# Sparse attention with a SwiGLU FFN: scores of two heads in two row tiles, one-hot sums, a 0/1 mask multiplied by VectorE, and a written order of key-tile steps

## The chip, the cores and the metric

The kernel runs on one core of one Trainium2 chip. The metric is device time in microseconds (us) of that core. Engines are named as in the profile: PE is TensorE (PEld its weight loads), DVE is VectorE, ACT is ScalarE, POOL is GpSimd, SP is SyncE. Every time quoted for a kernel is the median of its runs; executions of one kernel mostly agree within half a per cent (those of e3, e6 and e14 below differ by 1.3 to 1.5).

## The reference

Four batches of block-sparse attention (8 heads, 768 tokens, head size 64), then one RMS norm and a SwiGLU FFN over the 3072 tokens. Blocks are of 32 tokens; a key block is visible if it is a neighbour, the first or last row or column, or one of three sampled blocks.

```
scores = q @ k.T / 8, masked to -1e9 where the block is not visible
attn   = softmax(scores) @ v                       # (4, 8, 768, 64)
x      = attn as (3072, 512)
xn     = x / sqrt(mean(x*x) + 1e-6) * rms_g
out    = (silu(xn @ w_gate) * (xn @ w_val)) @ w_out   # 512 -> 1536 -> 512
```

## The kernel before

The mask is part of the contraction of the scores: each head's K and Q have 24 more rows, an indicator of the key block and a row of 0 or -1000 for each query. Masked scores come out of one matmul of 88 rows, and the exponential makes them zero. V has a 65th column of ones, so the A·V matmul also gives the row sums.

```
def attn_head(b, h, stage, e):
    for jt in range(NC):                       # 6 key tiles
        for ic in range(2):                    # 2 halves of 384 queries
            stp = pst.tile([P, 384], FP32, tag="stp")
            nc.tensor.matmul(out=stp, lhsT=KTf[0:64 + NB, sl, jt*P:(jt+1)*P],
                             rhs=QTf[0:64 + NB, sl, ic*384:(ic+1)*384], ...)
            nc.scalar.activation(out=ExpS[:, sle, jt*2 + ic, :], in_=stp, func=AF.Exp, scale=SCALE)
    # ... 36 matmuls: ExpS as weights, V and its ones column (65) moving; then 1/Z, the scaling
    # and six sums of squares on VectorE

def ffn_gateval(pool, g, f):                   # gate and value of one 128-wide FFN tile
    gp = pool.tile([P, TG], FP32, tag="gp");  vp = pool.tile([P, TG], FP32, tag="vp")
    # ... 4 matmuls into gp, 4 into vp ...
    nc.scalar.activation(out=th, in_=gp, func=AF.Tanh, scale=0.5)
    nc.vector.scalar_tensor_tensor(out=u, in0=th, scalar=1.0, in1=gp, op0=ALU.add, op1=ALU.mult)
    nc.vector.tensor_tensor(out=hp, in0=u, in1=vp, op=ALU.mult)
# ... the FFN of batch b-1 is written between the heads of batch b; the last batch's FFN stands
# alone, with gp and vp in pools of two buffers each
```

The program's text gives only a rough order. The framework's scheduler decides in which order each engine gets its instructions.

The softmax here doesn't subtract the row's maximum and nothing guards it: scores larger than these inputs give would overflow.

Of the kernel before, what the change touches and what calls it, by code (L numbers as in the profile page):

```python
# [8 lines left out]

FP32 = mybir.dt.float32
BF16 = mybir.dt.bfloat16
# [6 lines left out]
def kernel(  # L19
# [13 lines left out]
    P = 128  # L33
# [5 lines left out]
    NT = B * S  # L39
    MASKV = -1000.0  # L40
    SCALE = 1.0 / (D ** 0.5)
    NRND = sampled_blocks.shape[1]
    NF = DFF // P
    TG = 384
    NTT = TG // P

    const = ctx.enter_context(tc.tile_pool(name="const", bufs=1))
    persist = ctx.enter_context(tc.tile_pool(name="persist", bufs=1))
    raw = ctx.enter_context(tc.tile_pool(name="raw", bufs=4))
    work = ctx.enter_context(tc.tile_pool(name="work", bufs=3))  # L50
    stg = ctx.enter_context(tc.tile_pool(name="stg", bufs=10))
    ffw = ctx.enter_context(tc.tile_pool(name="ffw", bufs=3))
    attn_psum_stack = ExitStack()
    pst = attn_psum_stack.enter_context(tc.tile_pool(name="pst", bufs=2, space=bass.MemoryType.PSUM))
    pt = attn_psum_stack.enter_context(tc.tile_pool(name="pt", bufs=1, space=bass.MemoryType.PSUM))
    po = attn_psum_stack.enter_context(tc.tile_pool(name="po", bufs=1, space=bass.MemoryType.PSUM))
    pff = attn_psum_stack.enter_context(tc.tile_pool(name="pff", bufs=1, space=bass.MemoryType.PSUM))
# [4 lines left out]
    epsb = const.tile([P, 1], FP32, name="epsb")  # L62
    nc.vector.memset(epsb, 1e-6)
# [5 lines left out]
        base=1, pattern=[[-1, 32]], channel_multiplier=1,  # L69
    )  # L70
    nc.gpsimd.affine_select(
        out=Bm, in_=Bm, compare_op=ALU.is_ge, fill=0.0,
        base=1, pattern=[[1, 32]], channel_multiplier=-1,
    )
    for cm, base in ((1, 0), (1, -(NB - 1)), (0, 0), (0, -(NB - 1))):
        pat = [[1, 32]] if cm == 0 else [[0, 32]]
        nc.gpsimd.affine_select(
            out=Bm, in_=Bm, compare_op=ALU.not_equal, fill=1.0,
            base=base, pattern=pat, channel_multiplier=cm,
        )  # L80
    samp_i = const.tile([32, NRND], I32, name="samp_i")
    _sbt = sampled_blocks.tensor
    _sbt32 = _dc.replace(_sbt, dtype=I32, shape=tuple(_sbt.shape[:-1]) + (_sbt.shape[-1] * 2,))
    s64 = _sbt32.ap()
    nc.sync.dma_start(out=samp_i[0:NB, :], in_=s64[:, 0:2 * NRND:2])
    samp_f = const.tile([32, NRND], FP32, name="samp_f")
    nc.vector.tensor_copy(out=samp_f[0:NB, :], in_=samp_i[0:NB, :])
    jb_iota = const.tile([32, 32], I32, name="jb_iota")
    nc.gpsimd.iota(jb_iota, pattern=[[1, 32]], base=0, channel_multiplier=0)
    jb_iotaf = const.tile([32, 32], FP32, name="jb_iotaf")  # L90
    nc.vector.tensor_copy(out=jb_iotaf, in_=jb_iota)
    onehot = const.tile([32, 32], BF16, name="onehot")
    for r in range(NRND):
        nc.vector.tensor_tensor(
            out=onehot[0:NB, 0:NB],
            in0=samp_f[0:NB, r:r + 1].to_broadcast([NB, NB]),
            in1=jb_iotaf[0:NB, 0:NB], op=ALU.is_equal,
        )
        nc.vector.tensor_tensor(
            out=Bm[0:NB, 0:NB], in0=Bm[0:NB, 0:NB], in1=onehot[0:NB, 0:NB],  # L100
            op=ALU.max,
        )
    BmT = const.tile([32, 32], BF16, name="BmT")
    nc.vector.transpose(out=BmT, in_=Bm)

    Kind = const.tile([32, S], BF16, name="Kind")
    nc.gpsimd.memset(Kind, 1.0)
    nc.gpsimd.affine_select(
        out=Kind[0:NB, :], in_=Kind[0:NB, :], compare_op=ALU.is_equal, fill=0.0,
        base=0, pattern=[[1, NB], [0, 32]], channel_multiplier=-1,  # L110
    )
    Qmask = const.tile([32, S], BF16, name="Qmask")
    bmt_exp = BmT[0:NB, 0:NB].to_broadcast([NB, NB, 32])
    nc.vector.tensor_scalar(
        out=Qmask[0:NB, :], in0=bmt_exp,
        scalar1=-MASKV, scalar2=MASKV, op0=ALU.mult, op1=ALU.add,
    )

    NSLOT = 6
    NSLOTE = 2  # L120
    KTf = persist.tile([P, NSLOT, S], BF16, name="KTf")
    QTf = persist.tile([P, NSLOT, S], BF16, name="QTf")
    Vp = persist.tile([P, NSLOT, NC, 65], BF16, name="Vp")
    ExpS = persist.tile([P, NSLOTE, 12, 384], BF16, name="ExpS")
    for sl in range(NSLOT):
        nc.scalar.dma_start(out=KTf[64:64 + NB, sl, :], in_=Kind[0:NB, :])
        nc.scalar.dma_start(out=QTf[64:64 + NB, sl, :], in_=Qmask[0:NB, :])
        nc.vector.memset(Vp[:, sl, :, 64:65], 1.0)

    xbr = [persist.tile([P, NT], BF16, name=f"xbr{i}") for i in range(DM // P)]  # L130
    ssq = persist.tile([P, 2, NC], FP32, name="ssq")
    rstd = persist.tile([P, 2, NC], FP32, name="rstd")

    rmsg = const.tile([P, H // 2], FP32, name="rmsg")
    nc.sync.dma_start(out=rmsg, in_=moe_rms_g.rearrange("(h p) -> p h", p=P))

    wg = persist.tile([P, DM // P, DFF], BF16, name="wg")
    wv = persist.tile([P, DM // P, DFF], BF16, name="wv")
    wo = persist.tile([P, NF, DM], BF16, name="wo")
    nc.gpsimd.dma_start(out=wg, in_=moe_w_gate.rearrange("(c p) f -> p c f", p=P))  # L140
    nc.gpsimd.dma_start(out=wv, in_=moe_w_val.rearrange("(c p) f -> p c f", p=P))
    nc.gpsimd.dma_start(out=wo, in_=moe_w_out.rearrange("(c p) f -> p c f", p=P))
    nc.scalar.mul(out=wo, in_=wo, mul=0.5)

    hprods = {}

    def ffn_gateval(pool, g, f):
        gp = pool.tile([P, TG], FP32, name="gp", tag="gp")
        vp = pool.tile([P, TG], FP32, name="vp", tag="vp")
        for c in range(DM // P):  # L150
            nc.tensor.matmul(  # L151
                out=gp, lhsT=wg[:, c, f * P:(f + 1) * P],
                rhs=xbr[c][:, g * TG:(g + 1) * TG],
                start=(c == 0), stop=(c == DM // P - 1),
            )
        for c in range(DM // P):
            nc.tensor.matmul(  # L157
                out=vp, lhsT=wv[:, c, f * P:(f + 1) * P],
                rhs=xbr[c][:, g * TG:(g + 1) * TG],
                start=(c == 0), stop=(c == DM // P - 1),  # L160
            )
        th = ffw.tile([P, TG], BF16, name="th", tag="th")
        nc.scalar.activation(out=th, in_=gp, func=AF.Tanh, scale=0.5)  # L163
        u = ffw.tile([P, TG], BF16, name="u", tag="u")
        nc.vector.scalar_tensor_tensor(  # L165
            out=u, in0=th, scalar=1.0, in1=gp, op0=ALU.add, op1=ALU.mult,
        )
        hp = ffw.tile([P, TG], BF16, name="hp", tag="hp", bufs=2 * NF + 2)
        nc.vector.tensor_tensor(out=hp, in0=u, in1=vp, op=ALU.mult)  # L169
        hprods[(g, f)] = hp  # L170

    def ffn_out(pool, g, tt):
        yp = pool.tile([P, DM], FP32, name="yp", tag="yp")
        for f in range(NF):
            nc.tensor.matmul(  # L175
                out=yp, lhsT=hprods[(g, f)][:, tt * P:(tt + 1) * P],
                rhs=wo[:, f, :],
                start=(f == 0), stop=(f == NF - 1),
            )
        yo = ffw.tile([P, DM], FP32, name="yo", tag="yo")  # L180
        nc.scalar.copy(out=yo, in_=yp)  # L181
        nc.sync.dma_start(out=out[g * TG + tt * P:g * TG + (tt + 1) * P, :], in_=yo)

    def make_ffn_units(b, pool):
        units = []
        for g in (2 * b, 2 * b + 1):
            for f in range(NF):
                units.append((ffn_gateval, pool, g, f))
            for tt in range(NTT):
                units.append((ffn_out, pool, g, tt))  # L190
        return units

    def attn_pair_load(b, hp):
        sl0 = (b * H + 2 * hp) % NSLOT
        sl1 = (b * H + 2 * hp + 1) % NSLOT
        qraw = raw.tile([P, NC, 2, D], FP32, name="qraw", tag="qraw")
        kraw = raw.tile([P, NC, 2, D], FP32, name="kraw", tag="kraw")
        for e in range(2):
            nc.sync.dma_start(  # L199
                out=qraw[:, :, e, :],  # L200
                in_=q[b, 2 * hp + e].rearrange("(c p) d -> p c d", p=P))
            nc.sync.dma_start(  # L202
                out=kraw[:, :, e, :],
                in_=k[b, 2 * hp + e].rearrange("(c p) d -> p c d", p=P))
        qbf = work.tile([P, NC, 2 * D], BF16, name="qbf", tag="qbf")
        kbf = work.tile([P, NC, 2 * D], BF16, name="kbf", tag="kbf")
        nc.vector.tensor_copy(out=qbf, in_=qraw)  # L207
        nc.vector.tensor_copy(out=kbf, in_=kraw)
        for e, (raw_, bf) in enumerate(((qraw, qbf), (kraw, kbf))):
            dst = QTf if e == 0 else KTf  # L210
# [125 lines left out]
```

## Time and profile before

| | before |
|---|---|
| time, median | 437.4 us (436.01 to 437.44), 436.78 with the run beside the changed kernel |
| TensorE, VectorE, ScalarE busy | 83%, 56%, 55% of the span |
| first exponential, first FFN matmul | 55.1 us, 131.3 us |
| from the end of the last exponential to the end | 64.8 us |

Part 1 of the profile's page: busy time of each engine, its share, and its instructions.

```profile
span 436.2 us, 7564 instructions
...
PE 360.2 (83%) x2854; PEld 209.8 (48%) x2880; DVE 246.4 (56%) x821; ACT 241.7 (55%) x518; POOL 6.2 (1%) x19
```

TensorE is the busiest. Its busy time by itself is no measure of work, since matmuls are pipelined (in the timeline below one is 0.33 us long, and the next starts after 0.163); what counts is how far apart they start. The table of windows divides the span by stage. Columns: the window and its length, busy us (and instructions) of PE, PEld, DVE, ACT and POOL, the granted TensorE clock, the DMA share, GB/s.

```profile
0.00:55.00 55.00, 6.44 (x44) 4.26 (x45) 14.69 (x43) 6.61 (x2) 6.17 (x19) 1.00 1.07 192
55.00:125.00 70.00, 60.30 (x444) 34.37 (x442) 32.22 (x149) 47.30 (x106) 0.00 (x0) 0.90 0.64 126
125.00:372.00 247.00, 237.46 (x2056) 140.91 (x2080) 164.82 (x559) 167.82 (x375) 0.00 (x0) 0.99 0.14 37
372.00:436.00 64.00, 56.02 (x317) 30.22 (x316) 34.71 (x71) 19.92 (x36) 0.00 (x0) 0.97 0.10 37
```

The clock's column has a gap: this profile's record of the clock starts only at 104.6 us, and earlier stretches are printed as 1.00. The chain of waits shows otherwise (start us, us, what):

```profile
60.91 1.89 PE opsum L246 x31
...
150.67 1.00 PE opsum L246 x31
```

The same 31 A·V matmuls start 0.055 us apart at 60.9 us and 0.032 at 150.7: the first batch's attention ran at a lower clock too, about half by this ratio.

Four stages: a start with little TensorE work, one batch of attention alone, a dense mixed stage (237.5 of 247 us busy), and a last stage of FFN alone.

The costliest groups, by form (columns: line, engine, operation, shapes, count; busy us and mean ns of one; idle us just before them, and whom they waited for):

```profile
L238 ACT ACTIVATE ExpS<-stp 128x384 bf16<-128x384 f32 x384 | 171.1, 491 | 48.4 <-PE stp L232 33.8 <-DMA QTf<-Qmask 8.3 <-PE opsum L246 2.7
L232 PE MATMUL stp<-QTf,KTf 88*128 88x384 bf16 x384 | 126.5, 365 | 15.4 <-ACT ExpS L238 9.4 <-DMA QTf<-Qmask 3.4 <-DVE KTf L214 0.6
...
L259 DVE CUSTOM_DVE_ANT_0 junk<-stage,ssq 128x64 bf16<-128x64 bf16 x168 | 36.6, 277 | 0.3
```

The last stage in the timeline (start us, us, engine, line, what):

```profile
396.03 0.33 PE L151 MATMUL gp<-xbr_152,wg 128*128 128x384 bf16 x1
396.11 0.56 DVE L165 SCALAR_TENSOR_TENSOR u<-th,gp 128x384 bf16<-128x384 bf16 x1
...
396.68 0.33 PE L157 MATMUL vp<-xbr_152,wv 128*128 128x384 bf16 x1
...
396.88 0.49 ACT L163 ACTIVATE th<-gp 128x384 bf16<-128x384 f32 x1 [0.81 <-PE gp L151]
...
397.33 0.33 PE L151 MATMUL gp<-xbr_152,wg 128*128 128x384 bf16 x1
```

One FFN tile takes 1.30 us there (gate matmuls start at 396.03 and again at 397.33), exactly eight matmuls of 0.163 us. The tanh and the multiply on VectorE run beside them, for another tile.

### The profile page before, as it was taken

To read this page: it belongs to the slowest core of one execution; us is meant where nothing else is said; L and a number is where in the kernel's file an instruction comes from. 1 tells how busy PE (TensorE), PEld (TensorE's weight loads), DVE (VectorE), ACT (ScalarE), POOL (GpSimd) and SP (SyncE) were. 2 spreads that over 40 slices of the span, in tenths; PEclk is the share of its full clock that TensorE was granted. 3 is DMA by queue.
4 is the path that set the end of the run, shared out by engine and by line. 5 is a ranking of instruction groups with operands and counts; after the bars stand their busy time and mean duration, and the time that the engine had idled before them with its cause. 6 is when DMAs were issued, how large, how long until landed. Compare 5 with 4: busy or idle time off the path is not lost.

```text
span 436.2 us, 7564 instructions
## 1 busy us (share of the span) xinstructions
PE 360.2 (83%) x2854; PEld 209.8 (48%) x2880; DVE 246.4 (56%) x821; ACT 241.7 (55%) x518; POOL 6.2 (1%) x19
## 2 busy tenths in 40 slices
PE   0002288898879999999999999989999999789996
PEld 0001134554555654655555555546555555345552
DVE  0016534363476862766887648578665566657380
ACT  0003266667676666676777476767773867333331
POOL 5000000000000000000000000000000000000000
PEclk9999999999659999999999999999999999989999
DMA  7999986557470202211310111010001000100101
GB/s 124 208 203 207 221 165 136 99 107 148 90 146 20 54 23 90 62 29 44 94 30 20 44 53 34 2 50 24 2 2 50 24 2 2 73 2 0 74 0 72
DMA packets 82407, 30.80 MB, mean 71 GB/s; under 512 B 76452, under 2 KB 78276, under 8 KB 82372
## 3 DMA queue, kind: packets, MB, share of 16 engines
q1 hardware_dynamic: 79332, 25.18, 26.1%
q0 software_dynamic: 2608, 4.72, 5.9%
q10 hardware_dynamic: 432, 0.44, 0.4%
q8 instruction: 22, 0.36, 0.4%
q14 instruction: 13, 0.11, 0.1%
HBM read 28.31 MB, written 6.29 MB: 79 GB/s over the span
## 4 chain that ended last, share of the span: by engine, by line
PE 71%; ACT 9%; SPq 8%; DVE 7%; DMA 3%; issue 2%; ACTq 0%; DVEq 0%
PE stp L232 17%; PE gp L151 14%; PE vp L157 13%; PE yp L175 13%; PE opsum L246 11%; ACT ExpS L238 7%; SPq L220 3%; SPq L202 3%; PE tqk L213 2%; PE to L280 2%; SPq L199 1%; DVE junk L259 1%; DMA vraw<-in_v_dram 1%; ACT yo L181 1%; DMA QTf<-Qmask 1%
## 5 line engine op out<-in xcount | busy, mean ns | idle before, releaser
L238 ACT ACTIVATE ExpS<-stp 128x384 bf16<-128x384 f32 x384 | 171.1, 491 | 48.4 <-PE stp L232 33.8
L232 PE MATMUL stp<-QTf,KTf 88*128 88x384 bf16 x384 | 126.5, 365 | 15.4 <-ACT ExpS L238 9.4
L165 DVE SCALAR_TENSOR_TENSOR u<-th,gp 128x384 bf16<-128x384 bf16 x96 | 53.0, 552 | 58.9 <-ACT th L163 56.5
L246 PE MATMUL opsum<-Vp,ExpS 128*128 128x65 bf16 x1152 | 76.8, 209 | 1.4 <-ACT ExpS L238 1.2
L246 PEld LDWEIGHTS <-ExpS 128*128 128x128 bf16 x1152 | 56.5, 107 | 44.3 <-issue 24.6
L163 ACT ACTIVATE th<-gp 128x384 bf16<-128x384 f32 x96 | 47.1, 490 | 54.2 <-PE gp L151 53.9
L175 PE MATMUL yp<-wo,hp 128*128 128x512 bf16 x262 | 65.6, 379 | 3.2 <-ACT yo L181 2.6
L169 DVE TENSOR_TENSOR hp<-u,vp 128x384 bf16<-128x384 bf16 x96 | 52.8, 551 | 19.3 <-PE vp L157 12.8
L232 PEld LDWEIGHTS <-KTf 88*128 88x128 bf16 x384 | 39.0, 107 | 30.5 <-issue 14.5
L151 PEld LDWEIGHTS <-wg 128*128 128x128 bf16 x384 | 35.8, 98 | 29.2 <-issue 7.9
L157 PEld LDWEIGHTS <-wv 128*128 128x128 bf16 x384 | 36.2, 98 | 25.2 <-issue 3.0
L213 PE MATMUL tqk<-ident,qbf 128*128 128x128 bf16 x96 | 13.0, 263 | 37.4 <-DVE qbf L207 37.3
L175 PEld LDWEIGHTS <-hp 128*128 128x128 bf16 x288 | 27.7, 97 | 32.2 <-issue 4.5
L181 ACT COPY yo<-yp 128x512 f32<-128x512 f32 x24 | 14.1, 586 | 42.7 <-PE yp L175 40.7
L259 DVE CUSTOM_DVE_ANT_0 junk<-stage,ssq 128x64 bf16<-128x64 bf16 x168 | 36.6, 277 | 0.3
L151 PE MATMUL gp<-xbr_152,wg 128*128 128x384 bf16 x96 | 31.6, 329 | 2.5 <-DVE u L165 1.7
L157 PE MATMUL vp<-xbr_152,wv 128*128 128x384 bf16 x96 | 31.6, 329 | 0.6 <-DVE hp L169 0.3
L151 PE MATMUL gp<-xbr_155,wg 128*128 128x384 bf16 x96 | 31.5, 329 | 0.1
L157 PE MATMUL vp<-xbr_153,wv 128*128 128x384 bf16 x96 | 31.6, 329 | 0.0
L151 PE MATMUL gp<-xbr_153,wg 128*128 128x384 bf16 x96 | 31.6, 329 | 0.0
L157 PE MATMUL vp<-xbr_154,wv 128*128 128x384 bf16 x96 | 31.4, 328 | 0.0
L157 PE MATMUL vp<-xbr_155,wv 128*128 128x384 bf16 x96 | 31.4, 328 | 0.0
(53 smaller groups left out, 235.0 us busy)
## 6 DMA issues: line engine op xcount, KB each, us to landing
qraw<-in_q_dram SPq DMA_DIRECT2D x32, 192.0 KB, 3.7
kraw<-in_k_dram SPq DMA_DIRECT2D x32, 192.0 KB, 4.0
vraw<-in_v_dram SPq DMA_DIRECT2D x32, 192.0 KB, 3.1
out_dram<-yo SPq DMA_DIRECT2D x24, 256.0 KB, 2.0
wg<-in_moe_w_gate_dram POOLq DMA_DIRECT2D x1, 1536.0 KB, 12.8
wv<-in_moe_w_val_dram POOLq DMA_DIRECT2D x1, 1536.0 KB, 18.8
wo<-in_moe_w_out_dram POOLq DMA_DIRECT2D x1, 1536.0 KB, 27.9
KTf<-Kind ACTq DMA_DIRECT2D x6, 36.0 KB
```

What stands on the lines that cost most here:

```text
L151: nc.tensor.matmul(out=gp, lhsT=wg[:, c, f * P:(f + 1) * P], rhs=xbr[c][:, g * TG:(g + 1) * TG], start=(c == 0), stop=(c == DM // P - 1),)
L157: nc.tensor.matmul(out=vp, lhsT=wv[:, c, f * P:(f + 1) * P], rhs=xbr[c][:, g * TG:(g + 1) * TG], start=(c == 0), stop=(c == DM // P - 1),)
L163: nc.scalar.activation(out=th, in_=gp, func=AF.Tanh, scale=0.5)
L165: nc.vector.scalar_tensor_tensor(out=u, in0=th, scalar=1.0, in1=gp, op0=ALU.add, op1=ALU.mult,)
L169: nc.vector.tensor_tensor(out=hp, in0=u, in1=vp, op=ALU.mult)
L175: nc.tensor.matmul(out=yp, lhsT=hprods[(g, f)][:, tt * P:(tt + 1) * P], rhs=wo[:, f, :], start=(f == 0), stop=(f == NF - 1),)
L181: nc.scalar.copy(out=yo, in_=yp)
L213: nc.tensor.transpose(out=t_[:, c, :], in_=bf[:, c, :], identity=ident)
L232: nc.tensor.matmul(out=stp, lhsT=KTf[0:64 + NB, sl, jt * P:(jt + 1) * P], rhs=QTf[0:64 + NB, sl, ic * 384:(ic + 1) * 384], start=True, sto ...
L238: nc.scalar.activation(out=ExpS[:, sle, jt * 2 + ic, :], in_=stp, func=AF.Exp, scale=SCALE,)
L246: nc.tensor.matmul(out=opsum[:, it, 0:65], lhsT=ExpS[:, sle, jt * 2 + it // 3, (it % 3) * P:(it % 3 + 1) * P], rhs=Vp[:, sl, jt, :], start ...
L259: nc.vector.tensor_tensor_reduce(out=junk, in0=stage[:, it, e, :], in1=stage[:, it, e, :], scale=1.0, scalar=(0.0 if h == 0 else ssq[:, b ...
```

## The change

The intent: half the exponential instructions (two heads, 768 wide), two heads' scores at the same time in two row tiles of TensorE, A·V in two column tiles, row sums as matmuls with one-hot weights, a shorter lag of the FFN behind the attention (units of 384 queries and not of 768), and an order written by hand, in which each of 192 steps takes one key tile of two heads and about 0.97 us of FFN work. (A row tile is half the rows of TensorE's array, enough for a contraction of 64; a column tile is half or a quarter of its columns.) The mask goes out of the contraction: a 0/1 tile is multiplied onto the exponentials by VectorE. The core of the diff (cuts marked):

```
+    ctx.enter_context(tc.manual_schedule())
...
+    def load_w_chunk(i):                        # norm weight folded into the gate and value weights
+        for w, src, mul in ((wg, wgv, 1.0), (wv, wvv, 0.5)):
+            st = wst.tile([P, DM // P, FCH], FP32, name="wstage", tag="wstage")    # 2 buffers
+            nc.sync.dma_start(out=st, in_=src[:, :, f0:f0 + FCH])
+            for c in range(DM // P):
+                nc.vector.tensor_scalar(out=w[:, c, f0:f0 + FCH], in0=st[:, c, :], ...)
...
+    def qk_exp(n, jt):
+        s_ = ps_s.tile([P, 2, 512], FP32, name="s_", tag="s")
+        for e in range(2):
+            nc.tensor.matmul(out=s_[:, e, 0:TG],
+                lhsT=KT[64 * e:64 * e + 64, jt * P:(jt + 1) * P],
+                rhs=QT[64 * e:64 * e + 64, ic * TG:(ic + 1) * TG], start=True, stop=True)
+        nc.scalar.activation(out=ptiles[n][:, jt, :, :], in_=s_[:, :, 0:TG], func=AF.Exp, scale=SCALE)
+        if jt % 2:
+            nc.vector.tensor_tensor(out=pv, in0=pv, in1=Mk[...].to_broadcast([P, 2, 2, TG]), op=ALU.mult)
...
+    # av: 12 matmuls in two column tiles; zsum: 12 in four column tiles of 32; wsum: sum of squares
+    # norm_a .. norm_d: 1/Z and 1/rms as matmuls, nine small VectorE operations, a GpSimd power
...
+    def ff_g(u, f):
+        if u == NU - 1:
+            gv = ps_s.tile([P, 2, 512], FP32, name="gv", tag="s")     # gate and value: two halves
+            gp = gv[:, 0, 0:TG]
+        else:
+            gp = ps_f.tile([P, TG], FP32, name="gp", tag="gp")        # one buffer
+        # 4 matmuls, tanh on ScalarE, uu on VectorE
+    def ff_v(u, f):
+        vp = ps_f.tile([P, TG], FP32, name="vp", tag="vp") if gv is None else gv[:, 1, 0:TG]
...
+        at(s1 + 4, norm_a, u); at(s1 + 5, norm_b, u); at(s1 + 6, norm_c, u)     # one step apart
+        at(s1 + 7, norm_d, u, 0); at(s1 + 7, norm_d, u, 1)
+    for i in range(DFF // FCH):
+        at(5 + 4 * i, load_w_chunk, i)
```

## The prediction

> **What bounds the kernel now.** TensorE. It is busy 83% of 436.2 us (page, part 1); the chain of waits is 71% TensorE. By stage (table of windows): to 55 us TensorE works 6 us (q arrives at 26.9 us; ScalarE's queue waits 40.1 us on the K-indicator copies); from 55 to about 125 us the first batch's attention runs without FFN; to 372 us it is mixed, TensorE 93-97% busy; from 372 us only the last batch's FFN is left, 64 us. In the timeline FFN matmuls start every 0.163 us (384 columns), the 512-column ones every 0.22, and 31 A·V matmuls take 1.0 us. Started work is thus: scores 384x0.163=63, A·V 38, FFN 125+63, transposes 192x0.1=19: 308 us. The mixed stage holds three batches of attention and FFN, some 228 us, in 247: already dense.
>
> **What changes (estimates from those durations).**
> TensorE: scores in row tiles 192x0.19=36, A·V in column tiles 192x0.18=35, new one-hot sums 18+5, 384 small transposes 20-25, norm matmuls 15, FFN the same 188: about 320 us. It does *not* shrink. The Trainium skill's "TensorEngine Tiling (Array Packing)", Key Properties, says that changing the tiling mode drains TensorE; each step now changes it at least twice. No line of this profile shows its cost; I allow 0.05-0.1 us each, 25-45 us in all, part of it hidden in other waits.
> ScalarE: 384 exponentials of 384 (0.45 apart) become 192 of 768 (0.45+384x0.83 ns=0.77): 171 to 148; but evictions of A·V and K add 29; Sqrt table loads and the 5.3 us scaling of wo go. In all about 240.
> VectorE: the squares (36.6+15.2), stage and casts go; mask multiplies come, 96x0.95=91 (1536 elements at two per cycle, as the 0.55 us casts show, plus 0.15), weight folding 11, norm 35. In all about 250, as before.
> Neither is the bound, but both stand in strict order in the FFN chain: gate matmuls, tanh 0.49, u 0.55, then the single gate bank is free. With exponentials and mask multiplies ahead in the queue that takes about 2 us, against 0.8-1.5 us of other TensorE work: waits of 3-6 us per unit. The norm chain (nine small VectorE ops and a GpSimd power) adds 2 us per unit.
>
> **Critical path.** Gain: scores start near 19 us instead of 50; FFN starts near 60 us instead of 125 (held there by VectorE waiting for four weight chunks, 6-8 us of DMA each); the tail has half a batch, about 37 us instead of 64. In between lie 160 steps at 1.68 us of TensorE work = 269 us; with drains and waits 1.8-2.05, 290-330 us.
> Sum: 60 + 290..330 + 37 = 387..427; the ideal is 366. I lean to the lower end since the order looks tuned.
>
> **Predicted: 388 us, 350 to 425. Faster by over 2%: 0.85; within 2%: 0.09; slower: 0.06.**
>
> **What would show it.** Exponentials of 128x768 near 0.8 us; mask multiplies near 0.95; paired score matmuls starting almost together; VectorE idle on weight DMAs between 25 and 55 us; gate matmuls waiting on u; step period 1.8-2.0 us; from the last exponential to the end 35-40 us.
>
> **What would make it wrong.** Tiles that don't run together (zsum, A·V: +80 us, slower than before); drains near zero and a well-hidden gate chain (350 or less); a slower start from software-queue DMAs; a mask multiply at one element per cycle (1.75 us, VectorE the bound).

## The result, and the profile after

Ratios here are the mean time of one kernel's fast runs over that of the other's of the same rounds, so they differ a little from the ratio of the medians quoted.

| | before | changed |
|---|---|---|
| time, median | 436.78 us (436.01 to 437.44) | 488.81 us (487.64 to 490.6) |
| ratio | 1 | 1.1201 (95%: 1.1172 to 1.1231) |
| first exponential, first FFN matmul | 55.1, 131.3 us | 18.0, 77.5 us |
| last exponential's end to the end | 64.8 us | 60.6 us |

The result is right; the kernel is 12% slower. The prediction, 388 us with a range of 350 to 425, was wrong.

Part 1 of the page, and the table of windows by the stages of the changed kernel (start, attention alone, mixed, FFN alone):

```profile
span 485.7 us, 6795 instructions
...
PE 378.1 (78%) x2742; PEld 172.0 (35%) x2742; DVE 253.1 (52%) x441; ACT 236.5 (49%) x369; POOL 74.1 (15%) x112
```

```profile
0.00:18.00 18.00, 7.28 (x40) 2.99 (x41) 9.82 (x16) 2.08 (x2) 15.72 (x40) 1.00 0.76 102
18.00:77.50 59.50, 35.12 (x274) 14.45 (x273) 32.91 (x65) 29.33 (x42) 12.33 (x18) 0.71 0.73 162
77.50:425.00 347.50, 296.44 (x2216) 135.37 (x2213) 190.06 (x321) 193.71 (x304) 44.33 (x54) 0.98 0.16 32
425.00:485.60 60.60, 39.29 (x219) 19.23 (x216) 20.33 (x40) 11.41 (x23) 1.67 (x2) 1.00 0.07 26
```

TensorE, the fullest engine, is busy for 85% of the mixed stage, where it was 96% before. The mixed stage takes 347.5 us for 160 steps, 2.17 us each (predicted 1.8 to 2.05); the two others, 77.5 and 60.6 us, were predicted at 60 and 37. In the second stage the recorded clock averages 0.71. The Trainium skill's "TensorE: Matmul & The Clock Gate", Part 1, says that TensorE runs at half clock until it has been busy for some 3.4 us and falls back after an idle window; the trace agrees as far as it goes: 34 of the 52.7 us that it records at half clock lie in this stage, where TensorE waits. The record starts at 29.0 us, so the 1.00 of the first stage is not a measurement, and the two kernels' totals can't be compared.

The groups that answer to those of before:

```profile
L249 DVE TENSOR_TENSOR pt<-pt,Mk 128x1536 bf16<-128x1536 bf16 x96 | 91.5, 957 | 99.8 <-ACT pt L245 95.9
...
L363 PE MATMUL gp<-xn,wg 128*128 128x384 bf16 x336 | 68.6, 326 | 21.2 <-DVE uu L369 19.9
...
L367 ACT ACTIVATE th<-gp 128x384 bf16<-128x384 f32 x84 | 41.3, 492 | 39.2 <-PE gp L363 38.8
```

The mask multiply took 957 ns, as estimated (0.95). The exponentials of 768 took 0.81 us each in the timeline and start 0.70 us apart when back to back. Single costs were right; the waits were not. The chain of waits in part 4, before and then changed, by engine:

```profile
PE 71%; ACT 9%; SPq 8%; DVE 7%; DMA 3%; issue 2%; ACTq 0%; DVEq 0%
```

```profile
PE 46%; DVE 20%; ACT 18%; issue 7%; DMA 4%; POOL 2%; POOLq 0%; DVEq 0%; ACTq 0%
```

Of the chain that ended last, TensorE was 71% and is 46%; VectorE and ScalarE went from 16 to 38%. The view of waits (who waited for whom: us in total, times, longest us):

```profile
DVE pt L249 <- ACT pt L245: 95.9, 53, 5.9
...
PE gp L363 <- DVE uu L369: 19.9, 31, 1.4
...
PE gv L377 <- DVE uu L369: 14.0, 12, 1.2
...
PE s__430 L241 <- ACT KT L229: 11.8, 1, 11.8
...
PE ft L330 <- DVE FHL_190 L323: 10.3, 4, 3.3
...
PE ft L330 <- DVE FHL_191 L323: 7.1, 4, 2.2
```

The lines from the second on are TensorE's: gate matmuls that wait for u (the only gate bank, the buffer that TensorE writes them to, is still read), value matmuls of the last unit that wait for u, one wait of 11.8 us at the start, and the norm's matmul. The first line says that VectorE stands at the head of its queue 96 us for exponentials.

**The norm chain.** Unit 5's, from VectorE's sums to TensorE's matmul:

```profile
282.55 0.87 POOL L317 TENSOR_TENSOR rs<-ms,nhalf 128x3 f32<-128x3 f32 x1 [8.44 <-DVE ms L314]
283.46 0.18 DVE L319 TENSOR_TENSOR fx<-rz,rs 128x24 f32<-128x24 f32 x1 [0.99 <-POOL rs L317]
...
283.89 0.18 DVE L323 TENSOR_TENSOR FHL_190<-fx,FHL_190 128x24 bf16<-128x24 f32 x1
...
284.13 0.34 PE L330 MATMUL ft<-ident,FHL_190 128*128 128x128 bf16 x3 [2.23 <-DVE FHL_190 L323]
```

TensorE stands 2.23 us before its three transposes: the written order left one step between the chain's start and its use.

**The tail.** The last stage of the changed kernel:

```profile
456.27 0.49 ACT L367 ACTIVATE th<-gv 128x384 bf16<-128x384 f32 x1 [2.14 <-PE gv L363]
456.79 0.56 DVE L369 SCALAR_TENSOR_TENSOR uu<-th,gv 128x384 bf16<-128x384 bf16 x1 [0.62 <-ACT th L367]
457.40 0.81 PE L377 MATMUL gv<-xn,wv 128*128 128x384 bf16 x4 [1.17 <-DVE uu L369]
...
458.05 0.81 PE L363 MATMUL gv<-xn,wg 128*128 128x384 bf16 x4
...
458.89 0.49 ACT L367 ACTIVATE th<-gv 128x384 bf16<-128x384 f32 x1 [2.14 <-PE gv L363]
459.42 0.55 DVE L369 SCALAR_TENSOR_TENSOR uu<-th,gv 128x384 bf16<-128x384 bf16 x1 [0.62 <-ACT th L367]
```

One FFN tile now takes 2.63 us (u starts at 456.79 and at 459.42), where the same eight matmuls took 1.30 before. The value matmuls start 0.05 us after u has ended (456.79 + 0.56), although they don't need u: they write the other half of the tile whose first half u reads. Twelve tiles at 1.33 us too much are 16 us.

**The start.** VectorE from 25 to 45 us:

```profile
31.93 1.41 DVE L210 TENSOR_SCALAR wg<-wstage,gcol 128x384 bf16<-128x384 f32 x4 [6.02 <-DMA wstage<-in_moe_w_gate_dram]
...
38.18 1.41 DVE L210 TENSOR_SCALAR wv<-wstage,gcol 128x384 bf16<-128x384 f32 x4 [4.85 <-DMA wstage<-in_moe_w_val_dram]
39.51 1.82 DVE L249 TENSOR_TENSOR pt<-pt,Mk 128x1536 bf16<-128x1536 bf16 x2
41.24 0.55 DVE L228 COPY QT<-tqk 128x768 bf16<-128x768 bf16 x1
```

It waits 6.0 and 4.9 us for weight chunks; a mask multiply and the eviction of Q (L228, which the copy of K on ScalarE follows) stand behind, and TensorE waits 11.8 us for that copy.

**Mode changes.** Full-array gate matmuls, the scores' row tiles, full-array value matmuls, with nothing to wait for:

```profile
255.89 0.33 PE L363 MATMUL gp<-xn,wg 128*128 128x384 bf16 x1
...
256.15 0.34 PE L241 MATMUL s__2645<-QT,KT 64*128 64x384 bf16 x2
...
256.42 0.82 PE L377 MATMUL vp<-xn,wv 128*128 128x384 bf16 x4
```

The two score matmuls (x2) run at once: a run of 0.34 us is the length of one. But from the last gate matmul to them it is 0.26 us, and from them to the value matmuls 0.27, where a full-array matmul of 384 columns takes 0.163. So each change of tile mode costs 0.10 us. The Trainium skill's "TensorEngine Tiling (Array Packing)", Key Properties, says that a change of mode drains TensorE and gives no time; the trace agrees that it costs TensorE time, and by kind of change the median of those without a wait is 0.095 to 0.107 us.

**TensorE's account.** I took the starts of successive matmuls, counted 0.163 us for 384 columns (0.216 for 512) once for tiles that start together, 0.10 for each change of mode, and the rest as waiting:

| stretch | streaming | mode changes | waiting |
|---|---|---|---|
| before, mixed stage, 125 to 372 us | 210 us (85%) | none seen | 36 us (15%) |
| changed, units 5 to 8, 215 to 424 us | 142 us (68%) | 24 us (11%), 239 changes | 43 us (21%) |

A quarter of the second stretch, about one unit of 24 steps, is 52.3 us: 35.5 of streaming, 6.0 of changes, 10.8 of waiting. Over the whole span the same count gives some 293 us of streaming and 112 of waiting before, and 289 of streaming, 43 of mode changes (443) and 140 of waiting in the changed kernel.

### The profile page after: what moved, and what is told of

Same layout as the page of the kernel before. It is cut to its first block, busy times and chain, and to the rows that moved or that the text cites. A ratio compares the mean times of both kernels' runs of the same rounds, so it can differ in the third digit from the quotient of the medians.

```text
span 485.7 us, 6795 instructions
## 1 busy us (share of the span) xinstructions
PE 378.1 (78%) x2742; PEld 172.0 (35%) x2742; DVE 253.1 (52%) x441; ACT 236.5 (49%) x369; POOL 74.1 (15%) x112
## 4 chain that ended last, share of the span: by engine, by line
PE 46%; DVE 20%; ACT 18%; issue 7%; DMA 4%; POOL 2%; POOLq 0%; DVEq 0%; ACTq 0%
ACT pt L245 11%; PE yp L391 11%; DVE pt L249 7%; PE gp L363 7%; PE vp L377 6%; DVE uu L369 4%; PE zw L282 3%; ACT th L367 3%; DMA wstage<-in_moe_w_val_dram 3%; PE gv L377 2%; DVE hp L380 2%; ACT yo L397 2%; PE gv L363 2%; PE fb L344 1%; DVE QT L228 1%
## 5 line engine op out<-in xcount | busy, mean ns | idle before, releaser
L249 DVE TENSOR_TENSOR pt<-pt,Mk 128x1536 bf16<-128x1536 bf16 x96 | 91.5, 957 | 99.8 <-ACT pt L245 95.9
L363 PE MATMUL gp<-xn,wg 128*128 128x384 bf16 x336 | 68.6, 326 | 21.2 <-DVE uu L369 19.9
L377 PE MATMUL vp<-xn,wv 128*128 128x384 bf16 x336 | 68.6, 327 | 5.4 <-DVE hp L380 5.4
L369 DVE SCALAR_TENSOR_TENSOR uu<-th,gp 128x384 bf16<-128x384 bf16 x84 | 46.4, 552 | 47.8 <-ACT th L367 47.5
L380 DVE TENSOR_TENSOR hp<-uu,vp 128x384 bf16<-128x384 bf16 x84 | 46.4, 553 | 13.8 <-PE vp L377 9.4
L241 PEld LDWEIGHTS <-KT 64*128 64x128 bf16 x384 | 19.5, 94 | 85.7 <-issue 84.7
L229 ACT COPY KT<-tqk 128x768 bf16<-128x768 bf16 x16 | 12.8, 798 | 44.0 <-DVE QT L228 44.0
L264 PEld LDWEIGHTS <-vb 128*64 128x64 bf16 x384 | 21.5, 119 | 20.2 <-issue 12.0
L282 PE MATMUL zw<-pt,Ez 128*32 128x384 bf16 x384 | 22.9, 347 | 0.0
L347 DVE TENSOR_TENSOR xn<-osb,fb 128x768 bf16<-128x768 f32 x16 | 14.5, 948 | 1.5 <-PE fb L344 1.5
L380 DVE TENSOR_TENSOR hp<-uu,gv 128x384 bf16<-128x384 bf16 x12 | 6.6, 554 | 10.8 <-PE gv L377 10.8
```

What stands on the lines that cost most here:

```text
L241: nc.tensor.matmul(out=s_[:, e, 0:TG], lhsT=KT[64 * e:64 * e + 64, jt * P:(jt + 1) * P], rhs=QT[64 * e:64 * e + 64, ic * TG:(ic + 1) * TG] ...
L249: nc.vector.tensor_tensor(out=pv, in0=pv, in1=Mk[:, jt - 1:jt + 1, ic * TG:(ic + 1) * TG].unsqueeze(2).to_broadcast([P, 2, 2, TG]), op=ALU ...
L264: nc.tensor.matmul(out=o_[64 * e:64 * e + 64, 0:TG], lhsT=vb[:, 2 * pr + e, jt * D:(jt + 1) * D], rhs=pt_[:, jt, e, :], start=(jt == 0), s ...
L282: nc.tensor.matmul(out=zwt[u][32 * c:32 * c + 32, :], lhsT=Ez[:, pr, :], rhs=pt_[:, 2 * j2 + par, e, :], start=(pr == 0 and j2 == 0), stop ...
L363: nc.tensor.matmul(out=gp, lhsT=wg[:, c, f * P:(f + 1) * P], rhs=xns[u][:, c, :], start=(c == 0), stop=(c == NP - 1))
L369: nc.vector.scalar_tensor_tensor(out=uu, in0=th, scalar=1.0, in1=gp, op0=ALU.add, op1=ALU.mult)
```

## The experiments

Sixteen runs, three rounds each (the last two five). Theory: the parts of the change cost what they were said to cost, and the loss lies in new waits, made by the written order and by shared buffers, and in mode changes. Rivals: VectorE's mask work itself; row tiles; the written order as such; waits that hide one another, so that mending them gives nothing. Ratios are to the kernel before; the changed kernel has 1.1201.

| run | median us | ratio (95%) |
|---|---|---|
| e1 tail tiles apart | 471.9 | 1.0827 (1.0801 to 1.0853) |
| e2 norm later | 467.29 | 1.0718 (1.0701 to 1.0735) |
| e3 mask multiply later | 471.05 | 1.0798 (1.0741 to 1.0855) |
| e4 the scheduler's order | 438.67 | 1.0077 (1.0038 to 1.0117) |
| e5 336 more mode changes | 513.15 | 1.176 (1.1731 to 1.1789) |
| e6 its control | 494.4 | 1.1334 (1.127 to 1.1397) |
| e7 full-array scores | 510.49 | 1.1729 (1.1668 to 1.1791) |
| e8 no mask multiply (wrong result) | 455.87 | 1.0449 (1.0428 to 1.047) |
| e9 control of e7 | 511.81 | 1.1731 (1.1667 to 1.1795) |
| e10 weights early | 480.12 | 1.102 (1.0969 to 1.1071) |
| e11 four mends, written order | 417.58 | 0.9589 (0.9547 to 0.9631) |
| e12 scheduler, mended | 430.5 | 0.989 (0.9853 to 0.9926) |
| e13 e11 with the additive mask | 417.85 | 0.959 (0.9557 to 0.9624) |
| e14 e11 without a mask (wrong result) | 407.51 | 0.9361 (0.9334 to 0.9388) |
| e15 the kernel of e9 again | 511.07 | 1.1718 (1.1688 to 1.1748) |
| e16 the kernel of e7 again, same chip | 511.7 | 1.1738 (1.1712 to 1.1765) |

All but e8 and e14 gave the right result. The medians of e8 and e9 include one slow run each (463.73 and 530.38 us; without them 455.31 and 511.59); the ratios use fast runs alone.

### e1: tail tiles apart

```
-        if u == NU - 1:
-            gv = ps_s.tile([P, 2, 512], FP32, name="gv", tag="s")
-            gp = gv[:, 0, 0:TG]
+        if u == NU - 1 and f % 2:
+            gp = ps_s.tile([P, 2, 512], FP32, name="g2", tag="s")[:, 0, 0:TG]
+            gv = ps_s.tile([P, 2, 512], FP32, name="v2", tag="s")[:, 0, 0:TG]
         else:
             gp = ps_f.tile([P, TG], FP32, name="gp", tag="gp")     # value: the bank of vp
```

Two FFN tiles may be under way at once, as in the changed kernel; only gate and value are no longer halves of one tile.

> Changed kernel, but in the last unit gate and value go to separate tiles, alternating between the two FFN banks and the two score tiles. Main theory (of the 100 us miss, the tail's share is a dependency of the value matmuls on u, because both halves of one tile count as one; the tail then runs 2.63 us per FFN tile where the kernel before ran 1.30): period near 1.30 us, last exponential to end 60.5 -> 45 us, total 489 -> 473 +-3. Rival (the tail is bound by TensorE or by the tanh/u latency itself, not by the shared tile): period stays above 2.2 us, total within 3 us of 489.

It took 471.9 us, 17 less. VectorE's u in its tail:

```profile
445.68 0.55 DVE L370 SCALAR_TENSOR_TENSOR uu<-th,g 128x384 bf16<-128x384 bf16 x1
...
446.98 0.55 DVE L370 SCALAR_TENSOR_TENSOR uu<-th,gp 128x384 bf16<-128x384 bf16 x1
```

u comes every 1.30 us (445.68, 446.98). The last exponential ends at 425.9 and the kernel at 470.5: 44.6 us and not 60.6. The shared tile cost 16 to 17 us.

### e2: norm later

```
-            at(s1 + 6, norm_c, u);  at(s1 + 7, norm_d, u, 0);  at(s1 + 7, norm_d, u, 1);   LAG = 8
+            at(s1 + 8, norm_c, u);  at(s1 + 9, norm_d, u, 0);  at(s1 + 9, norm_d, u, 1);   LAG = 10
```

> Changed kernel with the last two parts of the norm chain emitted two steps later (FFN lag 10 instead of 8 steps). Main theory (TensorE stands 2.2 us per unit at the transpose matmul of the norm, waiting for nine small VectorE operations and the GpSimd power): that wait falls below 0.3 us per unit in seven units, and the total falls by 8-14 us; the last unit has nothing to fill the gap with. Rival (the gap is only moved: TensorE would wait elsewhere, on exponentials or on u, anyway): total within 4 us of 489.

It took 467.29 us, 21.5 less and more than I had expected. The view of waits no longer lists the norm's transpose behind VectorE among its larger entries, and the wait of gate matmuls on u fell from 19.9 to 14.7 us as well; why the other waits shrank with it was not tested (the edit also starts each unit's FFN two steps later). The rival falls.

### e3: mask multiply later

```
         # end of each step, after the FFN items
+        if step < NSTEP and step % 2:
+            mask_mul(step // NC, step % NC)      # taken out of qk_exp
```

> Changed kernel with each mask multiply emitted after the FFN work of its step instead of before it; same instructions, another order on VectorE. Main theory (VectorE waits in order for exponentials, 96 us in all, with u standing behind the mask multiply, and that holds the single gate bank): gate matmuls' wait on u falls from 19.9 us to below 10 and the total by 8-20 us. Rival (the gate bank waits for its own chain, tanh behind the exponential on ScalarE, whatever VectorE does): wait on u stays above 15 us and the total within 5 us of 489.

471.05 us, 18 less. TensorE's wait on u fell from 19.9 to 8.7 us, VectorE's wait for exponentials from 95.9 to 33.8. In this run the start got worse (first FFN matmul at 84.0 us, not 77.5), where the trace has mask multiplies behind two weight folds (43.5 to 46.2 us); the gain in the mixed stage, 325.8 us and not 347.6, was larger than the total shows.

### e4: the scheduler's order

```
-    ctx.enter_context(tc.manual_schedule())
```

> Changed kernel with one line taken out, the one that keeps the written order: the framework now orders each engine's instructions itself, as it did in the kernel before. Theory that the fixed order is the main cost (strict queues filled in the wrong order): total falls by 25 us or more, to 464 or less. Theory that buffers and their sharing are the cost (one gate bank, shared tail tile, mode changes): total between 475 and 500, and the tail keeps its 2.63 us period.

438.67 us: 50 less, by removing one line. All the instructions are there, in another order on each engine. The page's line for the gate matmuls (idle before them at the right):

```profile
L362 PE MATMUL gp<-xn,wg 128*128 128x384 bf16 x336 | 69.6, 328 | 1.7 <-DVE uu L368 0.6
```

The wait on u is 0.6 us where it was 19.9. From the first FFN matmul to the last exponential it takes 309 us and not 348, from there to the end 45.6 and not 60.6. The scheduler also gets round the shared tail tile: it runs two gates, then two values. The theory of the written order is the one that this run supports; my other statement, 475 to 500 us, is false. But e4 does not show that an order written by hand must be worse; e11 does the opposite. One thing got worse here: the scheduler put weight folds ahead of the mask's small operations, and the first exponential came at 34.0 us.

### e5 and e6: more mode changes, and the control

```
             for c in range(NP): ... gate (value) matmul ...
+            if c == 1 and gv is None:            # e5: 64 rows;  e6: 128 rows
+                nc.tensor.matmul(out=gpf[:, TG:TG + 32], lhsT=ident[0:64, :], rhs=Mk[0:64, 0, 0:32],
+                                 start=False, stop=False, skip_group_check=True)
```

> Changed kernel with a 32-column matmul of 64 rows put into the middle of each of 168 gate and value groups (all but the last unit's); it writes unused columns of their bank, so the result stays right. Each adds two changes of tile mode. In the changed kernel's trace a change costs 0.095-0.104 us of TensorE. Theory that such changes cost wall time as they stand: each insertion costs about 0.23 us, 336 changes x 0.1 = 34 us plus 168 x 0.03, less what falls into waits: total +20 to +40 us over 489, and at least 17 us above the control of the next run. Rival (the 0.1 us are only a gap that TensorE has to spare): within 8 us of the control.

> Control of the run before: the same inserted matmuls with all 128 rows, so no change of mode. About 0.03 us each: 489 +2 to +8 us by either theory.

513.15 and 494.4 us. The two differ only in the rows of 168 small matmuls, and by 18.75 us: 0.056 us of wall time for each of 336 added changes, a little over half of the 0.10 that TensorE loses at one. (e6's runs spread from 490.6 to 497.4 us, so this is uncertain by some 0.01.) The rest fell into waits: counted over the whole span as above, e5 has 779 changes and e6 443, 33 us more of them, and e5 waits some 10 us less. So mode changes cost wall time even in a kernel that waits so much, though not in full. The expected bound of 17 us was met, by less than the noise.

### e7, e9, e15, e16: scores on the full array, and the control

```
-                lhsT=KT[64 * e:64 * e + 64, ...], rhs=QT[64 * e:64 * e + 64, ...]
+                lhsT=KT[:, e, ...], rhs=QT[:, ...]     # K of head e, the other 64 rows zero
-        nc.scalar.copy(out=KTp[(b, pr)], in_=t_[:, 1, 0:S])                 # e9: only this part
+        for h in range(2):  nc.scalar.copy(out=KT[64h:64h+64, ...], in_=t_[64h:64h+64, 1, 0:S])
```

> Changed kernel with scores on the full array: K of each head in a tile of its own whose other 64 rows are zero, both heads' matmuls one after the other (0.163 us more of TensorE per step, 31 us in all), but fewer mode changes: about 1.3 fewer per step, 0.13 us. ScalarE gets 16 more copies of 0.8 us. Theory (two row tiles save no time, since the mode changes eat the saving): 489 +-10 us. Rival (two heads at once are a real gain of the change): +20 us or more, 509 or above.

It took 510.49 us, not 489 +-10, which speaks for the rival: row tiles a real gain. But that run has 16 more copies on ScalarE, so I ran the row tiles with the same copies:

> Control for the full-array scores, which took 510 and not 489 as I had said: row tiles as in the changed kernel, but K evicted by two copies of 64 partitions as in that run (16 more copies of 0.8 us on ScalarE). If the theory stands (TensorE's account of row tiles is even, and the 21 us came from the added ScalarE copies in a strict queue): 500 to 512, within 8 us of 510. If row tiles are a real gain of their own: 489 to 497.

511.81 us. But the runs of e9 had a lower granted clock than those of e7, one of them was slow (530.38 us at 0.81), so I ran both kernels again on one chip:

> The kernel of e9 (row tiles, K in two copies) once more, on the same chip as the next run, since e9's runs had a lower granted clock (0.916 to 0.929 in its fast ones) than e7's (0.934 to 0.946) and its profile was in the slow state. If the 22 us of e7 and e9 were the copies' and row tiles are even: 503 to 512, within 6 us of e16. If e9 was only slow by its clock and row tiles are a gain: 489 to 498, and e16 at least 12 us above.

> The kernel of e7 (full-array scores, same copies) once more beside e15: 508 to 512 by either statement.

511.07 and 511.7 us. The rival's 489 to 498 is out: the 22 us of e7 are the copies', and with the copies equal, scores in two row tiles and on the full array take the same time, within some 3 us. From 225 to 440 us TensorE's account has for e15 134 us of streaming, 23 of mode changes (229) and 58 of waiting, for e16 149, 10 (104) and 56. So two heads at once save nothing in this kernel: the 125 more changes of mode, about 1.35 for each of the 92 pairs of 384 columns, eat it. e15's clock was again the lower one, 0.912 to 0.935 against 0.933 to 0.943, with 88 us of its span recorded at half clock and 63 of e16's; why was not tested, nor whether row tiles would gain at equal clocks. And 12.6 us more work on ScalarE, busy half the time, cost 22 us: added work can cost more than its own length by what waits behind it in the queue.

### e8: no mask multiply

The multiply is moved into a function that nothing calls.

> Changed kernel without the mask multiplies (wrong result on purpose): 96 x 0.957 us less of VectorE. Main theory (VectorE is not the bound; the mask multiply costs only by its place in the strict queue, and running it later gave 18 us): total falls by 15 to 35 us, to 455-475. Rival (VectorE's 91 us of mask work are the cost of the change): total falls by 50 us or more, to the time of the kernel before or below.

455.87 us: 33 less for 91.5 us of VectorE work, inside what the theory gave; the kernel stays 4.5% slower than the one before. So the mask work is not the whole loss. How much of the 33 us is the work and how much its place in the queue is asked again in e14.

### e10: weights early

```
-        at(5 + 4 * i, load_w_chunk, i)                            # DMA and fold, two buffers
+        at(2 if i < 3 else 15, load_w_dma, i)                     # seven buffers
+        at(14 + 4 * i, load_w_chunk, i)                           # folds only
```

> Changed kernel with the weight chunks' DMAs issued at step 2 into seven buffers and folded at steps 14, 18, 22 and 26 instead of 5 to 17, so that VectorE need not stand at the head of its queue for them. Main theory (VectorE waits 14 us for weight DMAs there, and evictions, scores and the first FFN, at 77.5 us, stand behind it): TensorE's wait of 11.8 us for the K copy goes, FFN starts at 60-66 us, total 489 -> 472-478. Rival (what the start gains the mixed stage loses again, or DMA bandwidth sets the start): total above 483.

480.12 us, 9 less: between the two statements, nearer to the theory. The first FFN matmul came at 68.6 us and not 77.5, 8.9 us earlier, and the end by as much; the wait of 11.8 us went, but shorter waits of 1.1 to 3.6 us for the copy of K stayed. I had expected 60 to 66. What the start gains is not lost again later.

### e11: the four mends together

e1, e2, e3 and e10 in one kernel; the written order is kept.

> Changed kernel, fixed order kept, with four mends together: tail tiles apart, norm later, mask multiply later, weights early. If the losses are separate waits on the critical path they add up: 489 - 17 - 21 - 18 - 14 = 419 us, range 410-430, faster than the kernel before by 2 to 5%. If they hide one another: 435 or more.

417.58 us, where the sum of the four single gains gives 489 - 17 - 21.5 - 18 - 9 = 423. The losses add up, and to 6 us more than their sum: they were separate, on the critical path, and did not hide one another. This version beats both kernels: 4.1% faster than the one before, 15% than the changed one. Two lines of its view of waits:

```profile
DVE pt L260 <- ACT pt L252: 15.8, 15, 1.6
...
PE gp L375 <- DVE uu L381: 8.0, 24, 0.6
```

The first was 95.9, the second 19.9. By its own stages:

```profile
18.00:67.70 49.70, 35.03 (x279) 14.47 (x279) 31.86 (x65) 30.44 (x44) 14.78 (x19) 0.79 0.84 196
67.70:373.20 305.50, 285.81 (x2204) 131.73 (x2204) 187.57 (x321) 192.73 (x302) 41.81 (x52) 1.00 0.18 35
373.20:415.90 42.70, 38.28 (x223) 19.75 (x221) 20.78 (x41) 11.26 (x23) 1.68 (x2) 0.99 0.10 37
```

The mixed stage is 42 us shorter than in the changed kernel, the tail 18, the second stage 10. TensorE's account from 190 to 350 us: 77% streaming, 13% mode changes (205), 10% waiting. A unit takes 46.6 us by the starts of the exponentials, against 52.9 in the changed kernel.

### e12: the scheduler's order, mended

```
+            nc.vector.tensor_copy(out=wstg[(i, k)][0:1, 0, 0:1], in_=Mk[0:1, NC - 1, 0:1])   # DMA after the mask
```

with e1's tiles, e10's buffers, and without the line of the written order.

> The scheduler's order (438.7 us before) with two mends: weight DMAs held until the mask is made, so that the scheduler cannot put the weight folds ahead of it (first exponential at 34 us there, 18 us in the fixed order), and the tail tiles apart. Theory (start and tail add up): 438.7 - 14 - 4 = 421, range 412-428. If the start is set by weight DMA either way: 434-439.

430.5 us, 8 less than e4 and not 18. The first exponential came at 19.3 us and not 34.0, but the first FFN matmul only at 75.5 (81.9 in e4): the start is set by the weights there, which both statements had half. The written order, once mended, is better than the scheduler's by 13 us, but not by the order alone: in the profiles 7.8 us of the difference lie before the first FFN matmul (67.7 against 75.5), where e12 also holds the weight DMAs until the mask is made. From there to the last exponential the two take 305.5 and 308.6 us.

### e13 and e14: what the mask costs once the waits are mended

e13 puts 24 mask rows into the unused half of each head's full-array K and Q tile, drops the multiply, and evicts K and Q with four copies on VectorE (it also has five weight buffers, not seven, and issues the later weight DMAs at later steps); e14 only drops the multiply from e11.

```
-            if step < NSTEP and step % 2:  mask_mul(...)                     # both
+    KZ, QZ: [P, 2, S] per pair; rows 64 to 127 of head 0 and 0 to 63 of head 1: mask rows and zeros   # e13
+    lhsT=KZ[:, e, ...], rhs=QZ[:, e, ...]                                                     # e13
```

> On the combined kernel (417.6 us): the mask goes back into the contraction, as in the kernel before. Each head's K and Q lie in a full-array tile whose other 64 rows hold 24 mask rows and zeros; no mask multiply (96 x 0.957 us of VectorE less), evictions of K and Q as four copies of about 0.55 us on VectorE (ScalarE 12.8 us less). TensorE: +0.163 us per step for the second head, -0.13 for mode changes, +6 us in all. Theory (with the waits mended TensorE bounds, so the mask multiply is nearly free and this wins only what little waits are left): 408-420. Rival (the mask multiply is still a cost of its own through the VectorE queue): 400 or less.

> The combined kernel without the mask multiplies (wrong result on purpose); in the changed kernel taking them out gave 33 us. Theory (33 us were waits in a strict queue, of which running the multiply later already took 18, and the rest is now behind TensorE): 408-415, 3 to 10 us. Rival (a cost of its own): 395 or less.

417.85 and 407.51 us. Taking the multiply out gives 10 us in the mended kernel, where it gave 33 in the changed one: 23 of the 33 were waits that the mends, e3's above all, had already taken. What is left lies mostly at the start: in the profiles the first FFN matmul comes at 57.2 us in e14 and 67.7 in e11, and from it to the last exponential they take 301.9 and 305.5. Putting the additive mask back gains nothing. From 190 to 350 us it has 94 mode changes in place of 205, and 26.3 us of score streaming in place of 13.3: by this count again an even exchange, though e13 changes other things too.

## Why the prediction was wrong

**Right.** TensorE's work does not shrink. The costs of single instructions were right: mask multiply 957 ns (0.95 predicted), exponentials 0.81 us (near 0.8), score matmuls in pairs at the same time, VectorE idle on weight DMAs between 25 and 52 us, gate matmuls waiting on u. The multiply's rate of two elements per cycle agrees with the Trainium skill's "VectorE: DVE Perf Modes", Side-by-side, which gives tensor_tensor two at 16 bits and 0.96 GHz: by these figures an estimate for 1536 elements is 0.80 us, and the trace has 0.157 more. First scores near 19 us: 18.0.

**Wrong, by the terms of the sum "60 + 290..330 + 37 = 387..427".**

- *"the tail has half a batch, about 37 us"*: 60.6. I took over the 1.30 us per FFN tile of the kernel before and did not ask what the value matmuls wait for. They wait for u, since gate and value are halves of one tile; e1 shows 16 to 17 us. This is the step that failed in kind and not in size. The other 7 us (44.6 in e1 against 37) are size: between the last exponential and the last unit's first gate matmul, 425.1 to 442.3 us, stand its A·V, the previous unit's output matmuls and the norm chain.
- *"FFN starts near 60 us"*: 77.5. I had counted VectorE's wait for the weights, but not that Q's eviction, and through it K's and the scores, stand behind it. e10 gives 9 of the 17 us. The rest goes with the mask multiplies: without them too, in e14, the first FFN matmul comes at 57.2 us (one profile each).
- *"with drains and waits 1.8-2.05"* us per step: 2.17, 347.5 us and not 290 to 330. The streaming was less than I said (35.5 us per unit, 1.48 per step and not 1.68), which hid some 32 us of the miss over 160 steps. Mode changes were at the top of what I allowed (443, so 44 us at 0.10; 25 to 45 allowed), by luck, since nothing in the profile before shows their cost. The waits were well over (10.8 us per unit; 5 to 8 allowed). I had priced the gate chain and the norm chain, but not the VectorE queue in which the mask multiply waits for an exponential ahead of u. e3 gives 18 us by moving the multiply, e2 21.5 by moving the norm, and e14 shows that the multiply itself is worth 10, most of it at the start.
- *"I lean to the lower end since the order looks tuned"*: this took 19 us off the middle of my own sum (407), on no evidence in the profile. e4 shows the reverse: the same instructions in the scheduler's order take 438.7 us. That is still no less than the kernel before: e4 gains at the start and in the tail, but counted as above TensorE's streaming is the same (some 296 us against 293), and e4 has 543 mode changes, 53 us, where there were none. The written order spent what the change gains, and 52 us more.

Where the expected gain went: into new waits, each made by an instruction that stands in a strict queue ahead of what TensorE needs next. Undoing four of them brings 417.6 us. What is still missing to 388 is 30 us, of which 19 are my leaning to the lower end. The other 11 are in the start and the tail: e11's stages take 67.7, 305.5 and 42.7 us, where the sum has 60, 290 to 330 and 37. Mode changes don't explain them, since the sum allowed for them. They are large all the same: 390 in e11's mixed stage, 39 us at TensorE's own loss of 0.10 and 22 at the price that e5 and e6 found. That is an estimate from those runs; no run removes all of them.

**Left open.** Why e2 gave more than the norm's own wait of 17.4 us; which waits absorb part of an added mode change (0.056 us of time, 0.10 in the trace); and how much the half clock at the start cost.

## What to carry to other kernels

When a written order replaces a scheduler's, follow the chain that frees each single buffer and write down everything that stands ahead of it in each strict queue; a cheap operation that must wait for something else is dear there, and moving it later may give more than removing work. Ask of every pair of accesses to one tile whether the framework tells its parts apart. Before using row tiles of TensorE, count the changes of mode that they add: here a pair of 384 columns saved 0.163 us, and two changes took 0.20. They should pay where more work follows in the same mode, but no run here tests that.

## What the Trainium skill lacked or had wrong

- "TensorEngine Tiling (Array Packing)", Key Properties, says that a mode change drains TensorE but gives no time. Here it took 0.095 to 0.107 us on TensorE at full clock, and 0.056 us of kernel time for each one added (e5 against e6). Its Theoretical Speedup of up to 2 for contractions of 64 or less was no gain that e15 against e16 could show (511.07 and 511.7 us); most pairs stood between matmuls of another mode there.
- "TensorE: Matmul & The Clock Gate", Part 1, knows half clock, full clock, 13/16 and, as a fault, a quarter. The slow execution of e9 has a granted clock of 0.850 for 427 us of its span and half clock for 75, so a mean of 0.81, and took 530.38 us where the fast ones took 508 to 512. No run shows what caused it.
- No page prices a small GpSimd power: of 128x3 elements it took 0.87 us of the 2.8 us of a norm chain (281.32 to 284.13 us), in which eight VectorE operations took 0.17 to 0.31 us each.
